# Attention of the next block's first tile started one block early, and each tile's values' product put beside the next tile's scores

## The chip, the cores and the metric

One core of a Trainium2 chip. The time is device microseconds of one execution of the whole program; lower is better. A kernel's time is the median of its runs.

## The reference

Three layers in a row, all in float32. What is computed, cut to its core:

```python
# q, k, v: (4, 8, 576, 64)
scores = (q @ k.T) / 8                       # per batch and head
mask = (rel >= 0) & (rel < 64)               # a causal window of 64 positions
attn = softmax(where(mask, scores, -1e9))
x = (attn @ v) -> (4, 576, 512)
xn = (x - mean) / sqrt(var + 1e-6) * g_ln
x = x + relu(xn @ w_ch1) @ w_ch2             # 512 -> 2048 -> 512
xt = x.transpose(0, 2, 1)
u = x + (relu(xt @ tok1) @ tok2).transpose(0, 2, 1)
out = u + relu(u @ wb1) @ wb2                # 512 -> 1536 -> 512
```

## The kernel before, in words

The 2304 rows are 18 tiles of 128 rows, and 6 blocks of 3 tiles. The window is 64, so a tile of queries is two groups of 64 rows, each against 128 keys. Every instruction stands in the order in which it is written (`manual_schedule`), and each engine works through its own instructions in that order.

After an opening that does the attention of the first three tiles (`FIRST`), the loop `for i in range(NBLOCKS)` runs the first perceptron (`mlp_block("a", ...)`) over the blocks. A block has 16 steps. Step f is 12 matmuls into a PSUM tile `ha` (`mm1`, L350; PSUM pool `ps_h` with 2 places), a relu on ScalarE (L339) that also leaves room for a low part on VectorE (L340), then the step's hooks, then the 9 matmuls of step f-2 into three accumulators `acca` (`mm2`, L363). Steps 0 and 1 of a block have no `mm2`, and after step 15 the `mm2` of steps 14 and 15 follow.

The hooks carry the attention of the next block's tiles. For a tile t there are these operations:

- **S** (`tile_S`): 32 score matmuls on TensorE (L178) into two places of the PSUM pool `ps_a` (3 places), 8 masked maxima on VectorE (L191), 8 exponentials on ScalarE (L199).
- **T** (`tile_T_part`): 16 transposes of 32 rows on VectorE (L240); behind the 16th, the inverse of the sums (L221, L222).
- **V** (`tile_PV`): 32 matmuls with the values (L262) whose weights are what T wrote, scaling by the inverse on VectorE (L264), then `ln_scalar`: three passes on ScalarE (L280 to L282) that leave the centred rows `xh`.
- **X** (`xh_part`): 16 transposes of `xh` on VectorE (L333).

The table `STEPS` names, for the 15 steps 0 to 14, which of them stand in each step's hook: `T0*7` is seven pieces of T for the block's first tile. Block 1's hooks work for block 2, and so on; block 5 has none. Behind `mm1` of step 15 the callback `after` multiplies the transposed rows by the gain into `xnt` (`gained`, L316 on ScalarE, L317 on VectorE), from which the next block's `mm1` reads.

Block 0 is different (`lean`): its hooks transpose on TensorE (`att_T`), use the function `att_PV` by half tiles, and also turn the first perceptron's packed weights into two parts: `wnarrow` on VectorE (L110, L111) and `wsplit` on ScalarE (L92) and GpSimd (L93). In step 14 stand `ln_center` of tile 5 (L289) and the last `wnarrow`; in step 15 three transposes into `tpa` in three places of `ps_a`, and the last `wsplit`. Its `after` evaluates the gain from these PSUM tiles (`evac`), and between them makes a fourth `tpa`, which needs the first one's place again:

```python
                        for c in range(3):
                            evac(c)
                        trans("a", xh, i + 1, 3)
                        evac(3)
```

The pool `ap` has three SBUF places, which S, T and `wnarrow` share.

Of the kernel before, what the change touches and what calls it, by code (L numbers as in the profile page):

```python
# [9 lines left out]
F32 = mybir.dt.float32  # L10
# [7 lines left out]
P = 128  # L18
# [5 lines left out]
NH = H // 2  # L24
# [36 lines left out]
def mixer_kernel(ctx, tc, qT, kT, v, g, wa1, wa2, tok1, tok2, wb1, wb2, out):  # L61
# [140 lines left out]
    def att_T(u, first=False, copy=None):  # L202
        f_, sm = probs.pop(u), norm[u]
        if first:
            p_ = ps_h.tile([P, NH, P], F32, tag="h", name=f"pt{u}")
            s_ = hp.tile([P, 2 * N], F32, tag="hT", name=f"pts{u}")[:, 0:NH * P].rearrange("p (h c) -> p h c", h=NH)
        else:
            p_ = ps_a.tile([P, NH, P], F32, tag="a", name=f"pt{u}")
            s_ = sp.tile([P, NH, P], F32, tag="s", name=f"pts{u}")
        probsT[u] = s_  # L210
        for h in range(NH):
            nc.tensor.transpose(p_[:, h, :], f_[:, h, :], ident)  # L212
        if copy:
            copy(out=s_, in_=p_)
        else:
            nc.scalar.activation(out=s_, in_=p_, func=AF.Copy)
        if not first:
            inverse(sm)

    def inverse(sm):  # L220
        nc.vector.tensor_scalar_add(out=sm, in0=sm, scalar1=SM_EPS)  # L221
        nc.vector.reciprocal(out=sm, in_=sm)  # L222
# [11 lines left out]
    def tile_T_part(t, n):  # L234

        if n == 0:
            wholeT[t] = ap.tile([P, 2, NH, P], F32, tag="p", name=f"pts{t}")
        f_, s_ = (x[t].rearrange("p two h c -> p (two h) c") for x in (whole, wholeT))
        a, b = divmod(n, 4)
        nc.vector.transpose(out=s_[32 * b:32 * b + 32, :, 32 * a:32 * a + 32],  # L240
                            in_=f_[32 * a:32 * a + 32, :, 32 * b:32 * b + 32])
        if n == 15:
            del whole[t]
            for hh in range(2):
                probsT[2 * t + hh] = wholeT[t][:, hh]
            inverse(sums.pop(t))

    def tile_PV(t):
        del wholeT[t]
        for u in (2 * t, 2 * t + 1):  # L250
            probs.pop(u)
            att_PV(u)

    def att_PV(u):
        t, hh = divmod(u, 2)
        p_, r_ = probsT.pop(u), norm.pop(u)
        v_ = V[t].rearrange("p s (h d) -> p s h d", d=D)
        o_ = ps_a.tile([P, NH, D], F32, tag="a", name=f"o{u}")
        for h in range(NH):
            for s in range(2):  # L260
                r = slice(64 * s, 64 * s + 64)
                nc.tensor.matmul(o_[r, h], lhsT=p_[:, h, r], rhs=v_[:, s, hh * NH + h, :], start=True, stop=True)  # L262
        x_ = xt[t].rearrange("p (h d) -> p h d", h=H)
        nc.vector.tensor_tensor(out=x_[:, hh * NH:(hh + 1) * NH, :], in0=o_, in1=r_.to_broadcast([P, NH, D]),  # L264
                                op=ALU.mult)

    def ln_stats(t):
        st = stp.tile([P, 6], F32, tag="st", name=f"st{t}")
# [18 lines left out]
    def ln_center(t, eng=nc.vector):  # L287
        x_ = xh[t] = sp.tile([P, DM], F32, tag="s", name=f"xh{t}")
        eng.tensor_scalar(out=x_, in0=xt[t], scalar1=mv[t][:, 0:1], scalar2=None, op0=ALU.subtract)  # L289
# [92 lines left out]
    with tc.manual_schedule():  # L382
# [79 lines left out]
        def first_X(j, c):  # L462
            trans_tiles("a", xh, 0, c, (j,), ps_h if c == KD - 1 else ps_acc)

        fns = {"S": lambda t: att_S(t, True, True), "e": att_E, "D": dummies, "T": lambda u: att_T(u, True),
               "U": lambda u: att_T(u, True, nc.vector.tensor_copy), "V": att_PV,
               "L": ln_stats, "l": ln_scalar, "r": lambda t: inverse(sums.pop(t)), "N": ln_center, "k": wshrink, "n": wnarrow, "s": lambda _: wsplit(False),
               "X": lambda j: [first_X(j, c) for c in range(KD - 1)],
               "Y": lambda _: [first_X(j, KD - 1) for j in range(TPB)], "E": lambda c: evac(c)}
# [111 lines left out]
        def b_conv():  # L581
# [2 lines left out]

        STEPS = ("S0", "T0*7", "T0*8", "T0*1 S1", "V0 T1*3", "T1*8", "T1*5 X0*4", "S2 X0*2", "V1 X0*5", "T2*8",
                 "T2*8", "X0*5 X1*6", "V2 X1*5", "X1*5 X2*6", "X2*10")


        for i in range(NBLOCKS):
            hooks = {f: [] for f in range(FA + 2)}
            if i < NBLOCKS - 1:
                u0 = 2 * TPB * (i + 1)
                lean = i == 0

                def next_qk(t):
                    if t + 1 < NT:
                        place_fixed(t + 1)
                        load_qk(t + 1)  # L600

                def next_v(t):
                    if t + 1 < NT:
                        load_v(t + 1)

                for k in range(2 * TPB if lean else 0):
                    def s1(u=u0 + k):
                        new_x(u // 2)
                        att_S(u // 2, True)
                        next_qk(u // 2)  # L610

                    def s3(u=u0 + k):
                        att_PV(u)
                        if u % 2 == 1:
                            next_v(u // 2)
                            ln_stats(u // 2)

                    u, t, f = u0 + k, (u0 + k) // 2, 4 * (k // 2) + 1
                    if k % 2 == 0:
                        hooks[f].append(s1)  # L620
                    hooks[f + 2 + k % 2].insert(0, lambda u=u: att_T(u))
                    hooks[f + 3 + k % 2].append(s3)
                    if k % 2 == 1:
                        hooks[f + 5].append(lambda t=t: ln_center(t))

                def step(op, t, n):
                    if op == "S":
                        new_x(t)
                        tile_S(t)
                        next_qk(t)  # L630
                    elif op == "V":
                        tile_PV(t)
                        next_v(t)
                        ln_scalar(t)
                    else:
                        (tile_T_part if op == "T" else xh_part)(t, n)

                done = collections.Counter()
                for f, ops in enumerate(() if lean else STEPS):
                    for op in ops.split():  # L640
                        what, _, n = op.partition("*")
                        for _ in range(int(n or 1)):
                            hooks[f].append(lambda a=(what[0], TPB * (i + 1) + int(what[1]), done[what]): step(*a))
                            done[what] += 1

                def tr3(i=i):
                    for c in range(3):
                        trans("a", xh, i + 1, c)
                if lean:
                    hooks[FA - 1].append(tr3)  # L650

                def after(i=i):
                    if i > 0:
                        for c in range(KD):
                            for j in range(TPB):
                                gained(c, slice(j * P, (j + 1) * P), uts[TPB * (i + 1) + j][:, c])
                    else:
# [4 lines that stand above are left out]
            else:  # L662
                def ysk(k):
                    new_ys(0, k)
                    for t in range(2 * k, min(2 * k + 2, 9)):
                        y_split(t, nc.vector)
                hooks[0].append(lambda: b_load(3))
                for k in range(5):
                    hooks[k + LAG + 1].append(lambda k=k: ysk(k))
                for f in range(6 + LAG, 13 + LAG):  # L670
                    hooks[f - 0.5] = [b_narrow]
                    hooks[f].append(b_split)
                    if f != 7 + LAG:
                        hooks[f] += [b_narrow, b_shrink]
                hooks[13 + LAG].append(b_split)

                def after():
                    pass
            if i == 0:
                for f in range(FA):  # L680
                    if f < FA - 2:
                        hooks[f - 0.5] = [lambda: wnarrow(2)]
                    n = 1 if f > 0 and f % 4 in (0, 3) else 0
                    hooks[f] = hooks[f][:n] + [wsplit] + hooks[f][n:]
                hooks[FA - 2].append(lambda: wnarrow(2))
            acc = mlp_block("a", i, W, FA, xn, hooks, after)
            for j in range(TPB):
                t = TPB * i + j
                nc.vector.scalar_tensor_tensor(out=xt[t], in0=acc[j], scalar=mv.pop(t)[:, 1:2], in1=xt[t],
                                               op0=ALU.mult, op1=ALU.add)  # L690
# [153 lines left out]
```

## Time and profile before

| what | value |
|---|---|
| median of 3 runs | 833.75 us (833.71 to 833.81) |
| the profiled execution, its own time | 833.0 us |
| its span, first to last instruction | 830.8 us |
| TensorE busy | 817.2 us, 98% of the span |
| VectorE busy | 512.4 us, 62% |
| ScalarE busy | 284.5 us, 34% |
| GpSimd busy | 115.8 us, 14% |
| mean granted TensorE clock | 0.999 |

How to read it: PE is TensorE's matmuls, PEld its weight loads, DVE is VectorE, ACT ScalarE, POOL GpSimd. A busy share is an average over stages with different limits, so the timeline of the stage that changes says more than the share. The profiled execution's own time is 2.2 us longer than its span.

### The profile page before, as it was taken

The page shows a single profiled execution, that of the slowest core. Times are in us where ns is not written, and L with a number is a line of the kernel's source. Part 1 is how long each engine was busy: PE and PEld are TensorE (multiplying, and loading weights), DVE is VectorE, ACT ScalarE, POOL GpSimd, SP SyncE. Part 2 cuts the span into 40 slices and gives each one's busy share as a digit, 9 for nine tenths or more (in the row PEclk, how much of TensorE's full clock was granted, in tenths as well). Part 3 has the DMA queues.
Part 4 walks back from the last instruction along what each step waited for, and adds up shares of the span by engine and source line. Part 5 has one row for each costly group of instructions (what it writes and reads, how often), then busy time and mean ns, then how long its engine had stood idle before and what let it go on. Part 6 is the DMA issues. An engine that isn't in the chain of part 4 may idle for free.

```text
span 830.8 us, 12970 instructions
## 1 busy us (share of the span) xinstructions
PE 817.2 (98%) x5014; PEld 726.7 (87%) x5014; DVE 512.4 (62%) x1309; ACT 284.5 (34%) x765; POOL 115.8 (14%) x134
## 2 busy tenths in 40 slices
PE   7899999999999999999999999999999999999997
PEld 5888888888888898888999888999989999899996
DVE  5899877877787778678647458974433434434211
ACT  6877524235324333442245333432111111111110
POOL 2566500000000000000004352531000000000000
PEclk9999999999999999999999999999999999999999
DMA  9677212002100110212006400711001010000101
GB/s 342 233 263 262 100 59 64 33 20 90 58 26 28 59 56 26 96 40 64 1 0 194 130 1 26 253 51 39 1 0 39 1 39 1 12 27 1 39 1 38
DMA packets 23212, 58.36 MB, mean 70 GB/s; under 512 B 2800, under 2 KB 3568, under 8 KB 23152
## 3 DMA queue, kind: packets, MB, share of 16 engines
q1 hardware_dynamic: 19264, 43.66, 15.9%
q10 hardware_dynamic: 3888, 13.90, 4.8%
q8 instruction: 39, 0.64, 0.3%
q14 instruction: 21, 0.17, 0.1%
HBM read 52.82 MB, written 4.72 MB: 69 GB/s over the span
## 4 chain that ended last, share of the span: by engine, by line
PE 93%; DVE 1%; ACT 0%; issue 0%; ACTq 0%; DVEq 0%
PE acca L363 24%; PE ha L350 23%; PE hb L350 18%; PE accb L363 18%; PE td L722 3%; PE o L262 2%; PE s L178 2%; PE th L706 2%; DVE tmp L111 1%; PE king_offset=None)_1_5123 L706 0%; PE king_offset=None)_1_5174 L706 0%; PE king_offset=None)_1_4974 L706 0%; PE king_offset=None)_1_4939 L706 0%; DVE xs L796 0%; DVE tmp L110 0%; PE pt L212 0%
## 5 line engine op out<-in xcount | busy, mean ns | idle before, releaser
L350 PE MATMUL ha<-xnt,wa 128*128 128x384 f32 x1152 | 217.5, 337 | 1.6 <-POOL wa L93 1.6
L363 PE MATMUL acca<-wa,hTa 128*128 128x512 f32 x864 | 215.9, 396 | 0.0
L350 PEld LDWEIGHTS ha<-xnt,wa 128*128 128x128 f32 x1152 | 203.9, 188 | 10.0 <-POOL wa L93 2.2
L363 PEld LDWEIGHTS acca<-wa,hTa 128*128 128x128 f32 x864 | 159.0, 188 | 32.5 <-issue 1.7
L363 PE MATMUL accb<-wb,hTb 128*128 128x512 f32 x648 | 159.1, 392 | 0.0
L363 PEld LDWEIGHTS accb<-wb,hTb 128*128 128x128 f32 x648 | 120.7, 188 | 22.5
L340 DVE SCALAR_TENSOR_TENSOR hTb<-hb,hTb 128x384 fp32r<-128x384 f32 x72 | 40.1, 558 | 152.0 <-ACT hTb L339 151.9
L339 ACT ACTIVATE hTb<-hb 128x384 fp32r<-128x384 f32 x72 | 35.4, 492 | 237.0 <-PE hb L350 237.0
L339 ACT ACTIVATE hTa<-ha 128x384 fp32r<-128x384 f32 x96 | 46.6, 485 | 181.3 <-PE ha L350 181.1
L340 DVE SCALAR_TENSOR_TENSOR hTa<-ha,hTa 128x384 fp32r<-128x384 f32 x96 | 53.2, 555 | 86.9 <-ACT hTa L339 85.3
L240 DVE STREAM_TRANSPOSE pts<-f 32x256 f32<-32x256 f32 x192 | 83.6, 436 | 2.8
L350 PE MATMUL hb<-xnt,wb 128*128 128x384 f32 x432 | 80.5, 336 | 0.0
L350 PE MATMUL hb<-us,wb 128*128 128x384 f32 x432 | 80.5, 336 | 0.0
L350 PEld LDWEIGHTS hb<-xnt,wb 128*128 128x128 f32 x432 | 76.5, 188 | 2.6
L350 PEld LDWEIGHTS hb<-us,wb 128*128 128x128 f32 x432 | 76.5, 188 | 2.6
L333 DVE STREAM_TRANSPOSE xhT<-xh 32x128 f32<-32x128 f32 x192 | 57.9, 302 | 3.1
L199 ACT ACTIVATE f<-f,mx 128x128 f32<-128x128 f32 x120 | 46.5, 389 | 29.7 <-DVE mx L191 29.7
L325 DVE STREAM_TRANSPOSE ut<-xs 32x384 f32<-32x384 f32 x96 | 54.6, 569 | 1.9
L93 POOL TENSOR_TENSOR wa<-tmp,wa 128x512 fp32r<-128x512 f32 x32 | 45.2, 1432 | 30.2 <-ACT wa L92 30.2
L283 POOL TENSOR_SCALAR mv<-mv 128x1 f32<-128x1 f32 x13 | 2.9, 219 | 282.9 <-ACT xhT L282 282.9
L93 POOL TENSOR_TENSOR wb<-tmpb,wb 128x512 fp32r<-128x512 f32 x24 | 31.0, 1297 | 51.8 <-ACT wb L92 51.8
L111 DVE SCALAR_TENSOR_TENSOR tmp<-xs,tmp 128x512 uint32<-128x512 uint32 x32 | 26.9, 840 | 3.9 <-ACT xs L100 0.9
(110 smaller groups left out, 661.9 us busy)
## 6 DMA issues: line engine op xcount, KB each, us to landing
xs<-in_wa ACTq DMA_DIRECT2D x26, 512.0 KB, 4.4
qkv<-in_wb SPq DMA_DIRECT2D x20, 512.0 KB, 4.1
qkv<-in_v SPq DMA_DIRECT2D x28, 256.0 KB, 2.8
out<-xs SPq DMA_DIRECT2D x16, 256.0 KB, 2.4
qkv<-in_kT SPq DMA_DIRECT2D x10, 384.0 KB, 3.4
qkv<-in_qT SPq DMA_DIRECT2D x14, 256.0 KB, 2.8
xs<-in_wa SPq DMA_DIRECT2D x6, 512.0 KB, 8.1
more<-in_wb SPq DMA_DIRECT2D x4, 512.0 KB, 4.2
```

Source lines behind the costliest of these rows:

```text
L93: lo_engine.tensor_tensor(out=dst_lo, in0=src, in1=dst_hi.bitcast(F32), op=ALU.subtract)
L111: nc.vector.scalar_tensor_tensor(out=d, in0=w[:, :, 1], scalar=3, in1=low, op0=ALU.logical_shift_left, op1=ALU.bitwise_or)
L178: nc.tensor.matmul(s_[hh][64 * s:64 * s + 64, h], lhsT=Q[t][r, s, c], rhs=k_, start=True, stop=True)
L199: nc.scalar.activation(out=f_[:, h], in_=f_[:, h], func=AF.Exp, scale=-1.0, bias=mx[:, h], accum_out=sm[:, h])
L240: nc.vector.transpose(out=s_[32 * b:32 * b + 32, :, 32 * a:32 * a + 32], in_=f_[32 * a:32 * a + 32, :, 32 * b:32 * b + 32])
L325: nc.vector.transpose(out=d_[:, :, :, 32 * a:32 * a + 32], in_=s_[:, :, :, 32 * b:32 * b + 32])
L333: nc.vector.transpose(out=uts[t][32 * b:32 * b + 32, :, 32 * a:32 * a + 32], in_=s_)
L339: nc.scalar.activation(out=dst_hi, in_=src, func=AF.Relu)
L340: nc.vector.scalar_tensor_tensor(out=dst_lo, in0=src, scalar=0.0, in1=dst_hi.bitcast(F32), op0=ALU.max, op1=ALU.subtract)
L350: nc.tensor.matmul(h_, lhsT=w[:, a, cs], rhs=src[c][:, b], start=n == 0, stop=n == 3 * KD - 1)
L363: nc.tensor.matmul(acc[j], lhsT=t_[:, a, js], rhs=w[:, 2 + b, :], start=f == 0 and n == 0, stop=f == F - 1 and n == 2)
L722: nc.tensor.matmul(p_, lhsT=t2[tt][:, a, col:col + P], rhs=h1[b][:, tt, c], start=n == 0, stop=n == last)
```

## The change

A tile's two halves of the product with the values go into one PSUM tile of 512 columns instead of two of 256, and one VectorE instruction scales both. The table `STEPS` is new: V of a tile and S of the next tile stand in one step (2, 6 and 10). The first tile of each next block has its S in step 10 of the block before (`S3`) and the first 8 of its 16 T pieces in step 14 (`T3*8`); the other 8 stand in steps 0 and 1, four in each, and its V in step 2. For the first of these tiles, tile 6, S is put in step 13 of block 0 and 8 pieces of T in step 14, ahead of the `wnarrow` there. Counters of pieces are kept for each tile (`done`), across blocks.

```diff
-            inverse(sums.pop(t))
+            inverse(sums[t])
...
-            att_PV(u)
-
-    def att_PV(u):
-        t, hh = divmod(u, 2)
-        p_, r_ = probsT.pop(u), norm.pop(u)
+        att_PV(t, (0, 1))
+
+    def att_PV(t, halves):
+
         v_ = V[t].rearrange("p s (h d) -> p s h d", d=D)
-        o_ = ps_a.tile([P, NH, D], F32, tag="a", name=f"o{u}")
-        for h in range(NH):
-            for s in range(2):
-                r = slice(64 * s, 64 * s + 64)
-                nc.tensor.matmul(o_[r, h], lhsT=p_[:, h, r], rhs=v_[:, s, hh * NH + h, :], start=True, stop=True)
+        heads = slice(halves[0] * NH, (halves[-1] + 1) * NH)
+        o_ = ps_a.tile([P, len(halves) * NH, D], F32, tag="a", name=f"o{t}_{halves[0]}")
+        for n, hh in enumerate(halves):
+            p_ = probsT.pop(2 * t + hh)
+            for h in range(NH):
+                for s in range(2):
+                    r = slice(64 * s, 64 * s + 64)
+                    nc.tensor.matmul(o_[r, n * NH + h], lhsT=p_[:, h, r], rhs=v_[:, s, hh * NH + h, :],
+                                     start=True, stop=True)
         x_ = xt[t].rearrange("p (h d) -> p h d", h=H)
-        nc.vector.tensor_tensor(out=x_[:, hh * NH:(hh + 1) * NH, :], in0=o_, in1=r_.to_broadcast([P, NH, D]),
-                                op=ALU.mult)
+        r_ = norm[2 * t + halves[0]]
+        if len(halves) == 2:
+            r_ = sums.pop(t).rearrange("p two h one -> p (two h) one")
+        nc.vector.tensor_tensor(out=x_[:, heads], in0=o_, in1=r_.to_broadcast([P, len(halves) * NH, D]), op=ALU.mult)
...
-        STEPS = ("S0", "T0*7", "T0*8", "T0*1 S1", "V0 T1*3", "T1*8", "T1*5 X0*4", "S2 X0*2", "V1 X0*5", "T2*8",
-                 "T2*8", "X0*5 X1*6", "V2 X1*5", "X1*5 X2*6", "X2*10")
+
+        STEPS = ("T0*4", "T0*4", "V0 S1", "X0*6 T1*2", "T1*8", "T1*6", "V1 S2 X0*5", "X0*5 T2*4", "T2*8", "T2*4 X1*4",
+                 "V2 S3 X1*5", "X1*7", "X2*8", "X2*8", "T3*8")
+        done = collections.Counter()
...
+                if lean:
+                    hooks[FA - 3].append(lambda: step("S", 2 * TPB, 0))
+                    hooks[FA - 2] += [lambda k=k: step("T", 2 * TPB, k) for k in range(8)]
+                    done["T", 2 * TPB] = 8
...
-                        for _ in range(int(n or 1)):
-                            hooks[f].append(lambda a=(what[0], TPB * (i + 1) + int(what[1]), done[what]): step(*a))
-                            done[what] += 1
+                        a = what[0], TPB * (i + 1) + int(what[1])
+                        for _ in range(int(n or 1) if a[1] < NT else 0):
+                            hooks[f].append(lambda a=(*a, done[a]): step(*a))
+                            done[a] += 1
```

## Rows read from the trace of the kernel before

**Rows 1.** The chain that ended last: shares by engine (page); one piece of it in time.
```profile
PE 93%; DVE 1%; ACT 0%; issue 0%; ACTq 0%; DVEq 0%
...
406.19 6.26 PE ha L350 x36
```

**Rows 2.** Timeline, PE, block 1: start us, length us, instruction; a plain step, S, V.
```profile
133.33 2.27 PE L350 MATMUL ha<-xnt,wa 128*128 128x384 f32 x12
...
137.51 2.27 PE L350 MATMUL ha<-xnt,wa 128*128 128x384 f32 x12
...
142.92 2.27 PE L350 MATMUL ha<-xnt,wa 128*128 128x384 f32 x12
...
148.37 2.27 PE L350 MATMUL ha<-xnt,wa 128*128 128x384 f32 x12
```

**Rows 3.** Timeline, PE, block 0: half V beside S, then half V alone.
```profile
69.60 2.27 PE L350 MATMUL ha<-xnt,wa 128*128 128x384 f32 x12
...
75.63 2.27 PE L350 MATMUL ha<-xnt,wa 128*128 128x384 f32 x12
...
89.87 2.27 PE L350 MATMUL ha<-xnt,wa 128*128 128x384 f32 x12
...
94.86 2.27 PE L350 MATMUL ha<-xnt,wa 128*128 128x384 f32 x12
```

**Rows 4.** Timeline, PE, ACT and DVE, start of block 2; brackets: idle before, releaser.
```profile
183.03 2.27 PE L350 MATMUL ha<-xnt,wa 128*128 128x384 f32 x12
...
185.39 0.49 ACT L339 ACTIVATE hTa<-ha 128x384 fp32r<-128x384 f32 x1 [4.33 <-PE ha L350]
185.92 0.56 DVE L340 SCALAR_TENSOR_TENSOR hTa<-ha,hTa 128x384 fp32r<-128x384 f32 x1 [1.94 <-ACT hTa L339]
...
186.72 0.40 ACT L199 ACTIVATE f<-f,mx 128x128 f32<-128x128 f32 x1 [0.83 <-DVE mx L191]
...
189.81 0.47 ACT L339 ACTIVATE hTa<-ha 128x384 fp32r<-128x384 f32 x1
190.32 0.56 DVE L340 SCALAR_TENSOR_TENSOR hTa<-ha,hTa 128x384 fp32r<-128x384 f32 x1 [2.16 <-ACT hTa L339]
...
190.79 3.11 DVE L240 STREAM_TRANSPOSE pts<-f 32x256 f32<-32x256 f32 x7
...
194.53 3.60 DVE L240 STREAM_TRANSPOSE pts<-f 32x256 f32<-32x256 f32 x8
```

**Rows 5.** Timeline, DVE and ACT, block 2: V's scaling, the passes behind it, X.
```profile
173.99 3.16 DVE L333 STREAM_TRANSPOSE xhT<-xh 32x128 f32<-32x128 f32 x10
...
203.88 0.75 DVE L264 TENSOR_TENSOR xs<-o,sums 128x256 f32<-128x256 f32 x2
...
204.66 0.63 ACT L280 ACTIVATE xh<-xs 128x512 f32<-128x512 f32 x1 [1.29 <-DVE xs L264]
...
206.80 0.47 ACT L339 ACTIVATE hTa<-ha 128x384 fp32r<-128x384 f32 x1
```

**Rows 6.** Timeline, PEld, DVE and ACT, the end of block 0.
```profile
104.12 0.36 PEld L299 LDWEIGHTS tpa<-ident,xh 128*128 128x128 f32 x3 [0.17 <-DVE xnt L317]
...
96.69 0.18 DVE L271 BATCH_NORM_AGGREGATE mv<-st 128x2 f32<-128x6 f32 x1
...
98.22 0.48 DVE L289 TENSOR_SCALAR xh<-xs,mv 128x512 f32<-128x512 f32 x1
...
100.13 0.69 DVE L111 SCALAR_TENSOR_TENSOR tmp<-xs,tmp 128x512 uint32<-128x512 uint32 x1
...
103.45 1.67 DVE L317 SCALAR_TENSOR_TENSOR xnt<-tpa,gsb,xnt 128x384 fp32r<-128x384 f32 x3 [0.96 <-ACT xnt L316]
...
97.22 0.49 ACT L339 ACTIVATE hTa<-ha 128x384 fp32r<-128x384 f32 x1 [0.31 <-PE ha L350]
...
101.80 1.14 ACT L92 ACTIVATE wa<-tmp 128x512 fp32r<-128x512 f32 x2
```

**Rows 7.** Timeline, PE, the ten matmuls that open the kernel.
```profile
1.31 4.63 PE L388 MATMUL idle<-zero 128*128 128x512 f32 x10 [1.31 <-POOL zero L385]
```

More of the change, by code (lines that the diff above doesn't have):

```diff
@@ L465, in mixer_kernel @@
         fns = {"S": lambda t: att_S(t, True, True), "e": att_E, "D": dummies, "T": lambda u: att_T(u, True),
-               "U": lambda u: att_T(u, True, nc.vector.tensor_copy), "V": att_PV,
+               "U": lambda u: att_T(u, True, nc.vector.tensor_copy), "V": lambda u: att_PV(u // 2, (u % 2,)),
                "L": ln_stats, "l": ln_scalar, "r": lambda t: inverse(sums.pop(t)), "N": ln_center, "k": wshrink, "n": wnarrow, "s": lambda _: wsplit(False),
@@ L612, in s3 @@
                     def s3(u=u0 + k):
-                        att_PV(u)
+                        att_PV(u // 2, (u % 2,))
                         if u % 2 == 1:
@@ L636, in step @@
                         (tile_T_part if op == "T" else xh_part)(t, n)
-                done = collections.Counter()
                 for f, ops in enumerate(() if lean else STEPS):
```

## Prediction, made before the changed kernel ran

> **What bounds the kernel.** I read the chain that ended last first: TensorE is 93% of it [rows 1], so the kernel ends when TensorE has got through its list, and anything else counts only where TensorE stands still. Next, TensorE's timeline in block 1 [rows 2]: the starts of `mm1` follow each other by 4.18 us in a plain step (133.33 to 137.51), 5.41 us in a step with S and 5.45 us in one with V, and no wait for another engine is shown there. So an S lengthens its step by 1.23 us and a V by 1.27. Last, the timelines of VectorE and ScalarE where the new table puts work: the start of a block [rows 4], the passes behind V [rows 5] and the end of block 0 [rows 6]. The reader should look there for how long before TensorE needs a result its maker has it.
>
> **Gain: V beside S.** Both kinds of excursion leave the 128x128 matmuls and return. Block 0 has V and S side by side already: the step with half a V and an S takes 6.03 us (69.60 to 75.63), the one with half a V alone 4.99 (89.87 to 94.86) [rows 3]. S next to V therefore adds 1.04 us, where alone it adds 1.23: each joining saves 0.19 us. All 12 S of tiles 6 to 17 stand alone before and beside a V after: 12 x 0.19 = 2.3 us less. The bounds are 0 (a whole V leaves nothing to share) and 12 x 0.23 = 2.8.
>
> **Edits at nothing.** One scaling of 512 columns for two of 256: the two take 0.75 us together [rows 5], off TensorE's path. One PSUM place for a V with two for an S fill the three places of `ps_a`, each four steps old when it is needed again. The loads of q, k and v move with S and V and still have four steps, over 16 us. The X pieces of a block end in step 13 instead of 14; in their place stand 8 pieces of T, 3.6 us against the 3.16 us of ten X [rows 4, 5]. In step 14 that ends 0.7 + 0.47 + 3.6 = 4.8 us behind `mm1`'s end, just before the next relu part is due (4.18 + 0.7), so the gain behind it starts on time. If it were late by some tenths nothing follows: six us of `mm2` cover it.
>
> **Loss 1: V of each block's first tile now stands in step 2.** Its weights are what the 16th transpose writes, and eight of them stand behind the relu parts of steps 0 and 1 on VectorE. Count from the start of `mm1` of step 0. TensorE has three `mm1` in a row (steps 0 and 1 have no `mm2`): 6.26 us [rows 1], and with half of the 0.19 us that the two ends of an excursion cost it is ready for V at 6.35. In [rows 4] the block starts at 183.03; ScalarE's relu part begins 2.36 later, VectorE's 0.53 after that, at 2.89; VectorE is idle for 1.94 us ahead of it, waiting for ScalarE, so earlier work can't make it late, nor can the transposes behind it use that idle time. 0.47 later (190.32 to 190.79) the transposes begin, at 3.36. Eight take 3.60, so four take 1.8: 5.16. The relu part of step 1 comes next; seven transposes and such a part take 3.74 (190.79 to 194.53), which leaves 0.59 for the part: 5.75. Four more: 7.55. TensorE waits 7.55 - 6.35 = 1.2 us. Four blocks (1 to 4) have this step: 4.8 us. Bounds: 0.9 each (the step-0 part 0.06 earlier and both parts at 0.47, with nothing for the semaphore) to 1.4, so 3.6 to 5.6. What is late next: V, S and everything behind them on TensorE move by the same 1.2 us, so nothing gives it back.
>
> **Loss 2: S and half a T of tile 6 in block 0.** VectorE reaches S's maxima when the statistics of tile 5 end, at 96.87; ScalarE is free at 96.91, since it has 0.31 us idle before 97.22 [rows 6]. I put the first exponential at 97.15. Eight take 3.09 us (186.72 to 189.81) [rows 4], so ScalarE's relu part of step 14, before at 97.22, starts at 100.2, VectorE's 0.51 later at 100.7, and `ln_center` 0.47 later at 101.2 instead of 98.22: 3.0 us late. Now come 8 transposes, 3.6 us, and only then the last `wnarrow`, whose last instruction ended at 100.13 + 0.69 = 100.82: it ends at 100.82 + 3.0 + 3.6 = 107.4. ScalarE's second L92 needs that result, and the gain of the first `tpa` stands behind it on ScalarE. Of the two L92 in 1.14 us from 101.80, the second began about 102.35; L317 followed at 103.45, 1.1 later. So L317 begins at 108.5, and its first of three in 1.67 us ends 0.6 later, at 109.1. The fourth `tpa` waits for just that: its weight load at 104.12 already shows an idle 0.17 us on `xnt` L317 [rows 6], that is, this chain had no room even before. TensorE would be there at 104.12 + 1.04 (S of tile 6 now lies ahead) = 105.2 and waits 4.0 us. Queued behind it are `mm2` of steps 14 and 15 and all of block 1. Bounds: 2.5 (the exponentials one and a half us earlier) to 5.
>
> **Sum.** -2.3 + 4.8 + 4.0 = +6.5 us. Against the profiled execution's own 833.0 us that is 839.5; the median of the runs shown lies 0.75 us above that execution, so 840.2.
>
> **The clock.** The ten opening matmuls of 512 columns take 4.63 us [rows 7], 0.46 each; later ones of that width take half (a plain step's 4.18 less 6.26/3 for `mm1`, by nine, is 0.23). The mean granted clock was 0.999. Four us of standing still is more than the profile of before has anywhere after its start, and none of its rows shows what the granted clock (2.4 GHz there) does after one. If it fell to 1.2 GHz for as long as those ten matmuls took, about 2.3 us of work would be lost. The Trainium skill's page "TensorE: Matmul & The Clock Gate", section "HAM oscillation — how this bites in real kernels", says that gaps of a few us in TensorE's work let its clock fall to half and that the next work starts slow; by that rule the time would be the one of the fourth rival. No trace of before can show it.
>
> **Rivals.** A measurement of this kernel can tell about 0.2%, 1.7 us, from no change.
> - *Only the joining counts, faster.* The order on the queues would have to let all 16 transposes of a first tile, and the last `wnarrow`, end before TensorE comes. For it: VectorE has 1.94 us idle before the relu part of step 0. Against it: VectorE took its work in written order [rows 4], and with the four pieces of step 0 moved into the idle time the four behind step 1's part would still be late by almost a us. It decides where all waits together are under 0.6 us. Time: 833.75 - 2.3 = 831.5.
> - *The end of block 0 has room.* Against it: the 0.17 us wait that is there already. Time: 833.75 - 2.3 + 4.8 = 836.2.
> - *V in step 2 doesn't wait.* Against it: the sum above rests on rows of the same place. Time: 833.75 - 2.3 + 4.0 = 835.5.
> - *A further loss: the clock, a late V of the second tile, or no saving from joining.* The second tile's V: from the first V's start, scaling begins at 1.3 and takes 0.75; the three passes take 2.14 (204.66 to 206.80) [rows 5], the exponentials behind them 3.1, so the relu part of step 3 starts on ScalarE at 7.3 and VectorE's part 0.5 later, at 7.8; with 0.47, six X (1.9) and two T (0.9) 11.1; the part of step 4 is due at 11.4, and 0.47 and eight T end at 15.5; step 5's part is due at 15.6, with 0.47 and six T 18.8. TensorE comes 2.3 + 4 x 4.18 + 0.1 = 19.1 after. That is 0.3 us of room; the third tile has about 0.9 by the same count. A further 0.5 us on this chain would cost 4 x 0.2 = 0.8 us, the clock 2.3, no saving from joining 2.3: 841 to 842.5.
>
> **Chances.** The forecast with both losses 0.68, its own range 838.3 to 841.5 (block 0 from 2.5 to 5, the four waits from 3.6 to 5.6, taken together in part). The first rival 0.05, the second 0.07, the third 0.06, the fourth 0.14. The range has to hold 8 in 10: from 837.0 to 842.5 it takes in the forecast with the smaller prices and nearly all of the fourth. Faster by over 0.2% is the first rival without its mixed cases: 0.04. Within 0.2% (832.1 to 835.4) lies a part of the third: 0.04. Slower: 0.92.
>
> **What would show it.** Right: TensorE's V of step 2 in blocks 1 to 4 with 1.0 to 1.4 us of idle ahead of it, released by VectorE's L240; the fourth `tpa` at the end of block 0 with about 4 us of idle, released by L317; a joined step of 4.18 + 1.27 + 1.04 = 6.5 us without a wait. Wrong: no idle at one of these two places, a V in step 6 or 10 that waits for L240, or a granted clock below 2.4 GHz behind the long wait.

## The result: slower by 1.06%, and the profile after

The changed kernel takes 842.45 us (median of 5 runs, 841.53 to 843.18); the kernel before, run beside it, 833.71. The ratio is 1.0106 (95% interval 1.0094 to 1.0117), so the kernel became 8.8 us slower. From the prediction's start of 833.75 us that is 842.6 us. The forecast was 840.2, 6.5 us slower, in a range from 837.0 to 842.5: the measured time lies just above the upper end.

The table of waits of the profile after, TensorE's (engine, line, operation, what ended the wait: us in total, times, longest us), has two rows that have no like in the kernel before:

```profile
PE o L264 <- DVE pts L240: 4.0, 4, 1.0
PE tpa L304 <- DVE xnt L322: 3.9, 1, 3.9
```

The first is V of each block's first tile, four times, the second the end of block 0. In the changed kernel `mm1` is L355, `mm2` L368, V L264, the relu parts L344 and L345, the gain L321 and L322. TensorE's timeline of block 1, which answers to [rows 2]:

```profile
116.15 6.41 PE L355 MATMUL ha<-xnt,wa 128*128 128x384 f32 x36
122.49 0.33 PE L264 MATMUL o<-qkv,pts 128*64 128x64 f32 x2
123.83 1.15 PE L264 MATMUL o<-qkv,pts 128*64 128x64 f32 x30 [1.00 <-DVE pts L240]
124.90 1.10 PE L178 MATMUL s<-qkv 64*64 64x128 f32 x32
...
140.69 2.27 PE L355 MATMUL ha<-xnt,wa 128*128 128x384 f32 x12
142.89 1.15 PE L264 MATMUL o<-qkv,pts 128*64 128x64 f32 x32
143.97 1.10 PE L178 MATMUL s<-qkv 64*64 64x128 f32 x32
145.00 2.34 PE L368 MATMUL acca<-wa,hTa 128*128 128x512 f32 x9
147.18 2.27 PE L355 MATMUL ha<-xnt,wa 128*128 128x384 f32 x12
```

The reader should compare the two V. The second one, of the next tile, runs in 1.08 us (142.89 to 143.97) and its joined step takes 6.49 us (140.69 to 147.18), where the S step, 5.41, and the V step, 5.45, less a plain step, 4.18, make 6.68 [rows 2]: 0.19 us saved. The first one sets off on time at 122.49 with two of its 32 matmuls (the first eight transposes make the weights of 16 of them, those of the tile's first 64 queries), then stands: 2.41 us until S, 1.33 more than 1.08. The first tiles of blocks 2 to 4 take 1.32 to 1.33 more, too.

VectorE in the same stretch, which answers to [rows 4]:

```profile
119.02 0.56 DVE L345 SCALAR_TENSOR_TENSOR hTa<-ha,hTa 128x384 fp32r<-128x384 f32 x1 [1.92 <-ACT hTa L344]
119.61 1.78 DVE L240 STREAM_TRANSPOSE pts<-f 32x256 f32<-32x256 f32 x4
121.40 0.56 DVE L345 SCALAR_TENSOR_TENSOR hTa<-ha,hTa 128x384 fp32r<-128x384 f32 x1
121.97 1.80 DVE L240 STREAM_TRANSPOSE pts<-f 32x256 f32<-32x256 f32 x4
```

VectorE idles 1.92 us, takes the relu part of step 0 at 119.02 (2.87 us after the block's start at 116.15), and from there has no gap to speak of until the last transpose ends at 123.77; TensorE goes on 0.06 later.

The end of block 0, VectorE, ScalarE and TensorE, which answers to [rows 6]:

```profile
90.64 2.27 PE L355 MATMUL ha<-xnt,wa 128*128 128x384 f32 x12
...
101.51 0.56 DVE L345 SCALAR_TENSOR_TENSOR hTa<-ha,hTa 128x384 fp32r<-128x384 f32 x1 [2.16 <-ACT hTa L344]
...
102.38 3.57 DVE L240 STREAM_TRANSPOSE pts<-f 32x256 f32<-32x256 f32 x8
...
107.50 0.69 DVE L111 SCALAR_TENSOR_TENSOR tmp<-xs,tmp 128x512 uint32<-128x512 uint32 x1
108.11 0.55 DVE L345 SCALAR_TENSOR_TENSOR hTa<-ha,hTa 128x384 fp32r<-128x384 f32 x1
109.37 1.67 DVE L322 SCALAR_TENSOR_TENSOR xnt<-tpa,gsb,xnt 128x384 fp32r<-128x384 f32 x3 [0.70 <-ACT xnt L321]
...
108.23 0.63 ACT L92 ACTIVATE wa<-tmp 128x512 fp32r<-128x512 f32 x1 [0.43 <-DVE tmp L111]
...
103.86 2.31 PE L368 MATMUL acca<-wa,hTa 128*128 128x512 f32 x9
110.04 0.55 PE L304 MATMUL tpa<-ident,xh 128*128 128x128 f32 x3 [3.87 <-DVE xnt L322]
110.34 5.97 PE L368 MATMUL acca<-wa,hTa 128*128 128x512 f32 x18
```

The chain is the one that was walked: exponentials, relu part of step 14, eight transposes, `wnarrow`, L92, gain, and TensorE idle for 3.87 us. But the last row holds a second price. The 18 matmuls behind the wait last until block 1 begins at 116.15, 5.81 us. In the kernel before the same 18 took 4.22 us (104.47 to 108.69):

```profile
104.47 4.38 PE L363 MATMUL acca<-wa,hTa 128*128 128x512 f32 x18
108.69 2.27 PE L350 MATMUL ha<-xnt,wa 128*128 128x384 f32 x12
```

In the profile after, the windows of 2 us over this stretch (after the busy times: the granted clock, 1.00 being 2.4 GHz, then the DMA share and GB/s) say why:

```profile
108.00:110.00 2.00, 0.00 (x0) 0.00 (x0) 1.30 (x4) 1.77 (x4) 2.00 (x2) 1.00 0.00 0
110.00:112.00 2.00, 1.96 (x9) 1.64 (x10) 1.65 (x3) 0.86 (x2) 0.56 (x1) 0.82 0.03 8
112.00:114.00 2.00, 2.00 (x7) 1.51 (x6) 0.00 (x0) 0.00 (x0) 0.00 (x0) 0.50 0.00 0
114.00:116.00 2.00, 2.00 (x9) 1.64 (x8) 1.04 (x2) 0.00 (x0) 0.00 (x0) 0.83 0.00 0
116.00:118.00 2.00, 2.00 (x13) 1.95 (x12) 1.10 (x2) 0.00 (x0) 0.00 (x0) 1.00 0.00 0
```

TensorE stood still, and in the work that followed the granted clock was at its lower level, 1.2 GHz, for a little over three us: 1.6 us lost.

The trace's sum: joining -2.3, four V waits of 1.33 +5.3, the wait at the end of block 0 +4.0 (the fourth `tpa` begins at 110.04; without a wait it would have begun at 106.03, since the nine matmuls begun at 103.86 take 2.17 us, as in a joined step), the clock +1.6: +8.6 us, against 8.8 by the ratio. The profiled span is 9.5 us longer; the rest, 0.8 us, lies ahead of the steps that changed, since `mm1` of step 13 of block 0 begins at 90.64 instead of 89.87 [rows 3].

### The profile page after: what moved, and what is told of

It reads as the page before. It is cut to its first block, busy times and chain, and to the rows that moved or that the text cites. A ratio compares the mean times of both kernels' runs of the same rounds, so it can differ in the third digit from the quotient of the medians.

```text
span 840.3 us, 12940 instructions
## 1 busy us (share of the span) xinstructions
PE 819.3 (97%) x5014; PEld 730.1 (87%) x5014; DVE 513.6 (61%) x1297; ACT 284.2 (34%) x765; POOL 116.1 (14%) x134
## 4 chain that ended last, share of the span: by engine, by line
PE 84%; DVE 8%; ACT 3%; issue 0%; ACTq 0%; DVEq 0%
PE acca L368 21%; PE ha L355 18%; PE hb L355 18%; PE accb L368 18%; PE td L733 3%; DVE tmp L111 2%; DVE pts L240 2%; PE o L264 2%; PE th L717 2%; PE s L178 1%; DVE tmp L110 1%; ACT f L199 1%; DVE hTa L345 1%; ACT hTa L344 1%; ACT wa L92 0%
## 5 line engine op out<-in xcount | busy, mean ns | idle before, releaser
L355 PE MATMUL ha<-xnt,wa 128*128 128x384 f32 x1152 | 216.4, 337 | 1.5 <-POOL wa L93 1.5
L368 PE MATMUL acca<-wa,hTa 128*128 128x512 f32 x864 | 216.8, 397 | 0.0
L355 PEld LDWEIGHTS ha<-xnt,wa 128*128 128x128 f32 x1152 | 203.9, 188 | 9.5 <-POOL wa L93 2.1
L368 PEld LDWEIGHTS acca<-wa,hTa 128*128 128x128 f32 x864 | 160.6, 189 | 32.9 <-issue 2.4
L368 PE MATMUL accb<-wb,hTb 128*128 128x512 f32 x648 | 159.1, 392 | 0.0
L368 PEld LDWEIGHTS accb<-wb,hTb 128*128 128x128 f32 x648 | 120.7, 188 | 22.6
L345 DVE SCALAR_TENSOR_TENSOR hTb<-hb,hTb 128x384 fp32r<-128x384 f32 x72 | 40.1, 558 | 151.7 <-ACT hTb L344 151.6
L344 ACT ACTIVATE hTa<-ha 128x384 fp32r<-128x384 f32 x96 | 46.7, 487 | 211.7 <-PE ha L355 211.7
L344 ACT ACTIVATE hTb<-hb 128x384 fp32r<-128x384 f32 x72 | 35.4, 492 | 236.7 <-PE hb L355 236.7
L345 DVE SCALAR_TENSOR_TENSOR hTa<-ha,hTa 128x384 fp32r<-128x384 f32 x96 | 53.2, 555 | 88.7 <-ACT hTa L344 87.8
L240 DVE STREAM_TRANSPOSE pts<-f 32x256 f32<-32x256 f32 x192 | 83.7, 436 | 2.9
L355 PE MATMUL hb<-us,wb 128*128 128x384 f32 x432 | 80.5, 336 | 0.0
L355 PE MATMUL hb<-xnt,wb 128*128 128x384 f32 x432 | 80.5, 336 | 0.0
L355 PEld LDWEIGHTS hb<-us,wb 128*128 128x128 f32 x432 | 76.5, 188 | 2.6
L355 PEld LDWEIGHTS hb<-xnt,wb 128*128 128x128 f32 x432 | 76.5, 188 | 2.6
```

Of the source, the lines that this page charges most:

```text
L344: nc.scalar.activation(out=dst_hi, in_=src, func=AF.Relu)
L345: nc.vector.scalar_tensor_tensor(out=dst_lo, in0=src, scalar=0.0, in1=dst_hi.bitcast(F32), op0=ALU.max, op1=ALU.subtract)
L355: nc.tensor.matmul(h_, lhsT=w[:, a, cs], rhs=src[c][:, b], start=n == 0, stop=n == 3 * KD - 1)
L368: nc.tensor.matmul(acc[j], lhsT=t_[:, a, js], rhs=w[:, 2 + b, :], start=f == 0 and n == 0, stop=f == F - 1 and n == 2)
```

## The experiments

The theory: three separate prices (V in step 2, the order at the end of block 0, and a clock that falls because TensorE stands there), less what joining saves. The rivals: VectorE has no room anyhow, so that a wait only moves; the slow stretch has a cause of its own; joining saves nothing, or the single PSUM place is what costs. Each kernel was timed beside the kernel before; the times are medians of 4 to 11 runs.

**Eight transposes of tile 6 moved behind the gain.**

```diff
-                    hooks[FA - 2] += [lambda k=k: step("T", 2 * TPB, k) for k in range(8)]
...
                         evac(3)
+                        for k in range(8):
+                            step("T", 2 * TPB, k)
```

> The changed kernel with the 8 transposes of tile 6 taken out of step 14 of block 0 and put behind the last gain (evac of chunk 3). Theory (three separate prices: waits of V in step 2, the wait at the end of block 0 with a slower clock behind it, less what joining saves): the wait for the first gain falls from 3.87 us to under 1 us, the granted clock stays at 2.4 GHz, and the time falls by 4.9 to 5.6 us from 842.5, to about 837.2. V of tile 6 in block 1 still waits about 1.0 us. Rival (the exponentials of tile 6 on ScalarE are what delays the gain): at least 3 us of the wait stays, and the time is above 840.5.

Measured: 836.84 us, ratio 1.0037 (1.0025 to 1.0050), 5.6 us less than the changed kernel, the upper end of what the theory said. Its table of waits:

```profile
PE o L264 <- DVE pts L240: 4.0, 4, 1.0
...
PE tpa L304 <- DVE xnt L322: 0.2, 1, 0.2
```

TensorE's timeline at the same place:

```profile
106.44 4.34 PE L368 MATMUL acca<-wa,hTa 128*128 128x512 f32 x18
110.62 6.43 PE L355 MATMUL ha<-xnt,wa 128*128 128x384 f32 x36
```

The four V waits are untouched, the long one is 0.2 us, the clock read 1.00 in this stretch and the 18 matmuls take 4.18 us. The transposes in front of the gain were the cause of both the wait and the slow stretch; the exponentials, still in their place, were worth a few tenths.

**V and S one step later.**

```diff
-        STEPS = ("T0*4", "T0*4", "V0 S1", "X0*6 T1*2", "T1*8", "T1*6", "V1 S2 X0*5", "X0*5 T2*4", "T2*8", "T2*4 X1*4",
-                 "V2 S3 X1*5", "X1*7", "X2*8", "X2*8", "T3*8")
+        STEPS = ("T0*4", "T0*4", "T0*4", "V0 S1", "X0*6 T1*2", "T1*8", "T1*6", "V1 S2 X0*5", "X0*5 T2*4", "T2*8",
+                 "T2*4 X1*4", "V2 S3 X1*5", "X1*7 T3*2", "X2*8 T3*2", "X2*8 T3*2")
...
-                        for _ in range(int(n or 1) if a[1] < NT else 0):
+                        n = min(int(n or 1), 16 - done[a]) if a[1] < NT else 0
+                        for _ in range(n):
```

> The changed kernel with V and S of each step one step later (steps 3, 7, 11), the first tile's remaining transposes over steps 0 to 2, and 6 instead of 8 of them ahead in blocks 1 to 3. Block 0 is as in the changed kernel. Theory: V no longer waits for VectorE in any of blocks 1 to 4, which gives back 4 x 1.33 = 5.3 us: about 837.1, and each joined step is 6.5 us long. Rival (the waits only move, since VectorE has no room in a block): a V of the second or third tile waits instead, or mm1 waits for the relu parts, and the time stays above 840.

Measured: 837.07 us, ratio 1.0040 (1.0027 to 1.0052), 5.4 us less. No wait of V on L240 is left in its table of waits, and the long wait is as it was:

```profile
PE tpa L304 <- DVE xnt L322: 3.9, 1, 3.9
...
PE o L264 <- DVE pts L214: 1.6, 1, 1.6
```

The second row is an old one from the kernel's opening. The clock falls behind the long wait here as well (0.67 in the window from 108 to 112 us). VectorE has the room; only the order in the first three steps of a block lacked it.

**Both edits.**

> Both edits together. Theory: the two prices are independent, only the joining is left (12 x 0.19 = 2.3 us less than before) and at most 1 us of wait at the end of block 0: 831.4 to 832.5, which is 0.15 to 0.28% faster than before. Rival (joining saves nothing, or one PSUM place for a tile's values costs as much): 833.5 to 834.5, the same as before.

Measured: 831.67 us, ratio 0.9975 (0.9966 to 0.9985): 2.1 us faster than before. Removing both prices leaves what joining saves, and one wait of 0.45 us:

```profile
PE tpa L304 <- DVE xnt L322: 0.5, 1, 0.5
```

**The wait filled with work that nobody reads.** This kernel computes 16 products more than the reference asks for.

```diff
                             evac(c)
+                        d_ = ps_h.tile([P, DM], F32, tag="h", name="fill")
+                        for _ in range(16):
+                            nc.tensor.matmul(d_, lhsT=W[13][:, 0, 0:P], rhs=W[13][:, 1, :], start=True, stop=True)
                         trans("a", xh, i + 1, 3)
```

> The changed kernel with 16 matmuls of 512 columns, whose result nobody reads, on TensorE ahead of the fourth tpa at the end of block 0: at 0.23 us each 3.7 us, which just fills its 3.87 us wait. Theory (standing still is what lets the clock fall): the granted clock of the stretch behind stays at 2.4 GHz, the 18 matmuls there take 4.2 instead of 5.8 us, and the time falls by 1 to 2 us although work was added, to about 841; the runs lie closer together than the 841.5 to 843.2 of the changed kernel. Rival (the slow stretch has another cause, such as the weights that GpSimd is writing): 842 to 843 as before, or more.

Measured: 840.45 us, ratio 1.0082 (1.0068 to 1.0096), all runs between 840.30 and 840.79: 2.0 us less than the changed kernel, with more work; 1.6 of it lies in this stretch. TensorE at the end of block 0, and the windows of 8 us there (granted clock third from the end):

```profile
105.81 3.79 PE L673 MATMUL fill<-wa 128*128 128x512 f32 x16
109.80 0.55 PE L304 MATMUL tpa<-ident,xh 128*128 128x128 f32 x3 [0.20 <-DVE xnt L322]
110.10 4.34 PE L368 MATMUL acca<-wa,hTa 128*128 128x512 f32 x18
114.28 6.43 PE L355 MATMUL ha<-xnt,wa 128*128 128x384 f32 x36
```

```profile
104.00:112.00 8.00, 7.80 (x36) 6.19 (x35) 6.56 (x13) 3.26 (x6) 2.72 (x2) 1.00 0.01 3
112.00:120.00 8.00, 8.00 (x44) 7.59 (x43) 4.85 (x9) 0.98 (x2) 0.00 (x0) 1.00 0.00 0
```

The fourth `tpa` starts as late as in the changed kernel, but the 18 matmuls take 4.18 us (110.10 to 114.28) instead of 5.81. GpSimd writes its weights here as well (2.72 us busy in the first window), so that rival falls: the clock falls because TensorE stands still.

**One PSUM place alone.** The kernel before with the new `att_PV` and `tile_PV`, the old `STEPS` and nothing of tile 6 in block 0.

> The kernel before with one part of the change alone: one PSUM place and one scaling for a whole tile's values, with the old table of steps and nothing of tile 6 in block 0. Theory (this part is off TensorE's path): the same as before within 0.1%, 833.3 to 834.2, and a V of 32 matmuls still takes 1.08 us on TensorE. Rival (one place makes TensorE or VectorE slower, or frees a wait): 12 tiles by 0.1 us or more, so 1 us or more to either side.

Measured: 833.41 us, ratio 0.9994 (0.9986 to 1.0003): the interval holds 1, and a V of 32 matmuls takes 1.08 us as before. The interval excludes a loss of more than 0.3 us; it leaves room for a gain of up to 1.2. The next run shows that the gain of both edits isn't of this kind.

**S one step ahead of V.** On top of both edits:

```diff
-        STEPS = ("T0*4", "T0*4", "T0*4", "V0 S1", "X0*6 T1*2", "T1*8", "T1*6", "V1 S2 X0*5", "X0*5 T2*4", "T2*8",
-                 "T2*4 X1*4", "V2 S3 X1*5", "X1*7 T3*2", "X2*8 T3*2", "X2*8 T3*2")
+        STEPS = ("T0*4", "T0*4", "T0*4 S1", "V0", "X0*6 T1*2", "T1*8", "T1*6 S2", "V1 X0*5", "X0*5 T2*4", "T2*8",
+                 "T2*4 X1*4 S3", "V2 X1*5", "X1*7 T3*2", "X2*8 T3*2", "X2*8 T3*2")
```

> The run with both edits (e3_both, 831.7) with S taken apart from V again: S of the next tile stands one step ahead of V (steps 2, 6, 10 against 3, 7, 11). 11 of the 12 joinings go. Theory (each joining saves 0.19 us): 11 x 0.19 = 2.1 us more, 833.8, which is the kernel before again. Rival (the gain of e3_both comes from elsewhere): 831.2 to 832.2.

Measured: 833.62 us, ratio 0.9998 (0.9990 to 1.0007), 1.95 us above the run with both edits, 0.18 for each of the 11 joinings undone. Its trace has steps of 5.41 us with S and 5.45 us with V again. This kernel still has the single PSUM place and the earlier attention, and it is as fast as the kernel before: the gain of both edits is joining.

**Exponentials of tile 6 behind the relu part of step 14.** On top of both edits, `tile_S` of tile 6 leaves them out and step 14 begins with them:

```diff
                     hooks[FA - 3].append(lambda: step("S", 2 * TPB, 0))
+                    hooks[FA - 2] += [lambda u=u: att_E(u) for u in (4 * TPB, 4 * TPB + 1)]
```

> The run with both edits (e3_both) with the 8 exponentials of tile 6 put behind the relu part of step 14 of block 0 instead of ahead of it. Theory (they are the 3 us by which the relu parts of step 14 and all behind them on VectorE were late): the 0.45 us wait for the first gain falls to 0.2 or less as in the kernel before, 831.2 to 831.5. Rival (only the 8 transposes made it late): the wait stays at 0.45 us and the time at 831.7.

Measured: 831.20 us, ratio 0.9971 (0.9960 to 0.9981), the fastest here. TensorE's `tpa` matmuls no longer wait for the gain, as in the kernel before. ScalarE and VectorE in step 14:

```profile
98.68 0.49 ACT L344 ACTIVATE hTa<-ha 128x384 fp32r<-128x384 f32 x1 [1.35 <-PE ha L355]
99.07 0.39 ACT L199 ACTIVATE f<-f,mx 128x128 f32<-128x128 f32 x1
...
99.21 0.56 DVE L345 SCALAR_TENSOR_TENSOR hTa<-ha,hTa 128x384 fp32r<-128x384 f32 x1 [0.21 <-ACT hTa L344]
```

VectorE's relu part of step 14 starts at 99.21, 8.9 us behind the start of step 13 (90.29 in this run), instead of 10.9 in the changed kernel (101.51 less 90.64): the exponentials held it, as the walk said. That the total is below the run with both edits is within the spread of the runs; the wait that is gone is in the trace.

**`wnarrow` ahead of the eight transposes.** The changed kernel with the last `hooks[FA - 2].append(lambda: wnarrow(2))` put ahead of tile 6's T instead of behind it.

> The changed kernel with the last wnarrow of step 14 of block 0 ahead of the 8 transposes of tile 6 instead of behind them. If the wait for the first gain runs through the wnarrow, ScalarE's L92 and the gain behind it, as the prediction put it, and there is no second way, it falls by 3.6 us to under 0.5, the clock stays, and the time is about 837. If the relu part of step 15, which stands behind both in VectorE's queue ahead of the gain, holds it just as long, the wait falls by only 0.6 to 0.9 us to about 3.1: 840 to 842, with or without a slow clock behind it.

Measured: 841.18 us, ratio 1.0086 (1.0073 to 1.0100). The wait falls only to 3.06 us, and the clock still falls behind it (windows of 2 us):

```profile
109.85 0.70 PE L304 MATMUL tpa<-ident,xh 128*128 128x128 f32 x3 [3.06 <-DVE xnt L322]
...
105.11 3.57 DVE L240 STREAM_TRANSPOSE pts<-f 32x256 f32<-32x256 f32 x8
108.71 0.56 DVE L345 SCALAR_TENSOR_TENSOR hTa<-ha,hTa 128x384 fp32r<-128x384 f32 x1
109.19 1.66 DVE L322 SCALAR_TENSOR_TENSOR xnt<-tpa,gsb,xnt 128x384 fp32r<-128x384 f32 x3
...
105.76 1.50 ACT L321 ACTIVATE xnt<-tpa,gsb 128x384 fp32r<-128x384 f32 x3
```

```profile
110.00:112.00 2.00, 2.00 (x7) 1.68 (x7) 1.46 (x3) 0.58 (x1) 0.00 (x0) 0.53 0.03 8
112.00:114.00 2.00, 2.00 (x7) 1.56 (x6) 0.00 (x0) 0.00 (x0) 0.00 (x0) 0.62 0.00 0
```

So the way that the prediction named, through `wnarrow` and L92, is not the only one. ScalarE's part of the gain is early here, at 105.76. VectorE's part (L322) has to stand behind the transposes and the relu part of step 15 in VectorE's own queue, until 109.19, and this way holds the gain nearly as long.

## Why the prediction was right in its two waits and short by the clock

- **Joining, -2.3:** right. 0.19 in the step of the trace, 0.18 from undoing 11 of them.
- **The edits at nothing:** right; the single place alone makes no difference that can be measured (833.41 against 833.74, and the interval holds 1).
- **V in step 2, +4.8:** the place and the chain were right, the size is 5.3, 1.33 instead of 1.2 for each of the four. The walk let the transposes start 0.47 us after the relu part of step 0, and the trace shows 0.59 (119.02 to 119.61). With its other steps a little shorter than walked, the last transpose ends at 7.62 after the block's start instead of 7.55, and TensorE goes on 0.06 later.
- **The end of block 0, +4.0:** right, 4.0, and not by luck: with the 0.77 us by which step 13 starts later taken off, the last `wnarrow` ends at 107.4, as walked, and the gain begins at 108.6 instead of 108.5. Its account was incomplete: a second way, VectorE's own queue, is only 0.8 us shorter than the one named. And "no room even before" was too strong: `wnarrow` ended at 100.82 and the second L92 that reads it began about 102.35, 1.5 us later. That room and the 1.04 us of S on TensorE are why the exponentials' 3.0 us alone cost only 0.2 to 0.5.
- **The clock:** this is the step that failed. It was kept out of the sum, as part of the fourth rival at 0.14 with a price of 2.3, because no row of before showed a stand of that length. In the profile after it fell, which the prediction had named as a sign of being wrong, at a price of 1.6 us (5.81 against 4.22). The price of 2.3 had let the low clock last as long as the ten opening matmuls, 4.63 us; the windows show a little over three. With the 1.6 and the 0.5 by which the V waits were too small, 840.2 becomes 842.3. Filling the stand brought the time to 840.45, which is near the forecast, the time of a kernel whose clock stays; that it is as near as 0.25 us is luck in part, since the V waits still cost 0.5 more there than forecast. The Trainium skill's page "TensorE: Matmul & The Clock Gate", section "HAM oscillation — how this bites in real kernels", says that a gap of a few us in TensorE's work lets the clock fall to half; the traces agree: the clock fell behind the waits of 3.87 us (in the changed kernel and with V one step later) and of 3.06 us, and in none of them behind the V waits of 1.0 us. The 4.0 us of standing still in the sum should have drawn the clock's term in after it.
- **Later V:** right; V in steps 6 and 10 did not wait, in spite of only 0.3 us of room.

## What to carry to other kernels

Where one engine sets the end, an operation moved earlier is paid in the queue of the engine that makes its input: walk that queue from the last point at which it is known to be idle, and look for each later item in the same queue that somebody waits for. A wait of 3 or 4 us on TensorE cost more than its length here, since the matmuls behind it ran at the lower clock; waits of 1.0 us did not. A change that came out slower can hold a real gain: moving eight transposes and tile 6's exponentials at the end of block 0, and V and S one step later in the other blocks, turned 1.0106 into 0.9971.

## What the runs showed of the hardware that was not expected

Joining two excursions from the 128x128 matmuls to the smaller tiles saves 0.18 to 0.19 us, so that is what leaving and coming back cost together. Going from V's shape to S's within one excursion costs nothing that the rows show: S takes 1.03 us behind V (143.97 to 145.00), and 1.04 alone, in the profile before:

```profile
139.71 1.10 PE L178 MATMUL s<-qkv 64*64 64x128 f32 x32
140.75 2.33 PE L363 MATMUL acca<-wa,hTa 128*128 128x512 f32 x9
```

The clock also falls in the kernel's opening, in some of the profiled executions and not in others. In the profile after, the windows of 20 us there read (granted clock third from the end):

```profile
0.00:20.00 20.00, 14.86 (x195) 11.42 (x196) 10.52 (x65) 12.07 (x53) 4.19 (x21) 0.98 0.94 337
20.00:40.00 20.00, 18.21 (x157) 16.40 (x156) 17.03 (x42) 16.07 (x38) 11.09 (x10) 0.94 0.66 232
```

In the profile before they read 1.00. That can explain at most about half of the 0.8 us by which step 13 of block 0 starts later after: in the runs with V one step later and with the exponentials later these windows read 1.00 too, and step 13 still starts at 90.23 and 90.29, 0.4 us later than before. What makes the rest is open. Over the five runs of the changed kernel the mean granted clock goes with the time: 0.998 in the two fastest (841.53 and 841.98 us), 0.995 in the middle one, 0.993 in the two slowest (843.15 and 843.18); how much of this is the opening and how much the stand at the end of block 0 the runs without a trace leave open.
